# A range test on converted weights: two ScalarE passes with a sum, or one VectorE minimum

## The chip, the cores and the metric

The kernel runs on one core of one Trainium2 chip. Its time is the device time of one execution in microseconds (us). Three runs of the kernel before took 1075.24, 1077.2 and 1079.67 us, median 1077.2. A profile records one execution: the span is the time from its first to its last instruction, and the execution's own time is a little longer.

## The reference

The reference is an attention over hash buckets, followed by a Fourier mixing block with a small network. Reshapes and the bridge between the blocks are left out here.

```python
# q, k, v: (4, 8, 768, 64); proj: (64, 6)
q_bits = (einsum('bhsd,dk->bhsk', q, proj) > 0)          # k_bits likewise
bucket = sum(bits * 2 ** arange(6))
scores = where(q_bucket == k_bucket, q @ k.T / sqrt(64), -1e9)
x = softmax(scores) @ v                                  # to (4, 768, 512)

mixed = real(fft(fft(x, axis=1), axis=2))
u = x + mixed
un = (u - mean(u)) / sqrt(var(u) + 1e-6)
out = u + maximum(un @ w_ch1, 0) @ w_ch2                 # (512, 2048), (2048, 512)
```

The inputs w_ch1 and w_ch2 are float64. The kernel gets them as 64-bit integers and must turn them into float32 itself.

## The kernel before

**Stages.** The four batches are worked through one after another. In each, eight heads are taken as four pairs, and a pair's 768 keys as six chunks of 128. A chunk is scored on TensorE (L909), passed through exp on ScalarE (L922), masked on VectorE by comparing buckets (L936), summed on VectorE (L1043) and multiplied with the values on TensorE (L947). After a pair, the sums go to VectorE for a reciprocal (L979 to L982), are spread by small ScalarE copies (L990), turned back on VectorE (L995) and applied (L999). The mixing block of a batch (`mix`) then folds x on VectorE (L1124 to L1142), does the two Fourier steps on TensorE (L1164, L1193) and runs the network `mlp7`. While one batch is in its mixing block, the attention of the next is interleaved with it.

**The network.** Both matrix products are done with seven block products instead of eight (Strassen and Winograd). `inner` computes the hidden layer: for each of eight rows f it runs the seven products (L1473). ScalarE copies the results out of PSUM (L1513, L1516, L1523, L1528, L1532, L1540), and VectorE adds them up (L1517, L1524, L1529, L1533, L1541). ScalarE's Relus (L1496) are held back and issued right behind later copies. PSUM has two banks for these products, so a late copy stops TensorE. For batch 0 the left operands come from w1 in SBUF, and `quarters` (L1266 to L1269) prepares those of the next row on VectorE. `outer7` does the second product (L1352) with additions on VectorE (L1337, L1338, L1364, L1372, L1380, L1398 to L1404) and copies on ScalarE (L1371, L1382, L1385).

**The weights.** A float64 is two 32-bit words. `narrow` makes float32 out of a slice of 128x512 raw values: VectorE shifts and masks the high words (L639, L643), ScalarE scales the low words (L647), and VectorE adds the two (L649 or L652). The result is only right for numbers within the range of float32, so the kernel tests the range. If the test or another check fails, the whole computation is repeated by a slower general path, `_any_scores`, behind a branch at the end. In the kernel before, the test is two ScalarE instructions (L654 and L655): the absolute value of the high word as a number, and the Relu of a limit minus that value, summed over the slice into one column of the tile `strange`. Any sum above zero means that a word lies below the limit. L654 overwrites the high words in place when there is no other room, as for w2, so it comes behind VectorE's L643, which reads them.

w1 has 16 slices, converted while batch 0's attention runs. w2 has 16 slices as well (`weights2`), two for each step of `inner` of batch 0, and each half of them in one pass through `inner`. Two raw buffers are refilled by POOL's DMA queue (L704) as they come free. After every second slice VectorE forms four more blocks out of the converted ones (L1318 to L1321). Near the end, L1627 takes the maximum over `strange`, and it goes into the flag that decides on the branch.

**Order.** A part of the program up to the end of batch 0's attention is issued in the order in which it is written. Everything later is ordered per engine by a planner, which has costs of its own for the instructions and puts each into a fixed place in its engine's queue. `in_turn` makes an instruction follow the latest ones that `done_by` holds for each engine. Each engine then works through its queue strictly in that order and waits where an operand isn't ready.

Of the kernel before, what the change touches and what calls it, by code (L numbers as in the profile page):

```python
# [11 lines left out]
F32 = mybir.dt.float32  # L12
BF16 = mybir.dt.bfloat16
I32 = mybir.dt.int32
I64 = mybir.dt.int64
U32 = mybir.dt.uint32
AF = mybir.ActivationFunctionType
ALU = mybir.AluOpType
AX = mybir.AxisListType
# [5 lines left out]
DFF = 4 * DM  # L25
# [5 lines left out]
NDC = DM // P  # L31
GTT = 2
GT = GTT * P
WC = 512
# [451 lines left out]
def _main(  # L486
# [13 lines left out]
    nc = tc.nc  # L500
# [13 lines left out]
    def wt(shape, dtype, tag, name, bufs=2):  # L514
        return work.tile(shape, dtype, tag=tag, name=name, bufs=bufs)
# [4 lines left out]
    def pt(shape, name):  # L520

        turn[0] += 1
        if roomy[0] and turn[0] % 2:
            if turn[0] % 4 == 1:
                return ps_o.tile(shape, F32, tag="o", name=name)
            return ps_sc.tile(shape, F32, tag="sc", name=name)
        return ps_1.tile(shape, F32, tag="ps", name=name)
# [92 lines left out]
    w2 = const.tile([P, NFC, DM], F32, tag="w2", name="w2")  # L620


    least = const.tile([P, 1], F32, tag="least", name="least")
    nc.gpsimd.memset(least, float(897 << 20))
    strange = const.tile([P, 2 * NDC * DFF // WC], F32, tag="strange", name="strange")
    nc.gpsimd.memset(strange, 0.0)

    def narrow(dst, raw, col, low=None):


        lo, hi = (raw[..., i] for i in range(2))
        t = lo.bitcast(F32)
        if low is None:

            low, t = lo, hi.bitcast(F32)
        di = dst.bitcast(I32)


        nc.vector.tensor_scalar(  # L639
            di, hi, 3, (1 << 30) - 1,  # L640
            op0=ALU.logical_shift_left, op1=ALU.bitwise_and,
        )
        nc.vector.scalar_tensor_tensor(  # L643
            di, hi, -(1 << 30), di, op0=ALU.bitwise_and, op1=ALU.bitwise_or
        )

        nc.scalar.activation(low, lo.bitcast(U32), AF.Copy, scale=2.0**-29)  # L647
        if len(di.shape) == 2:
            nc.vector.tensor_tensor(di, di, low, op=ALU.add)  # L649
        else:  # L650
            for i in range(di.shape[1]):
                nc.vector.tensor_tensor(di[:, i], di[:, i], low[:, i], op=ALU.add)  # L652

        nc.scalar.activation(t, hi, AF.Abs)  # L654
        nc.scalar.activation(  # L655
            t, t, AF.Relu, bias=least, scale=-1.0, accum_out=strange[:, col : col + 1]
        )
# [17 lines left out]
    def centre(f, avg):  # L675
        for c in range(NDC):
            w = w1[:, c, f : f + WC]
            nc.vector.tensor_tensor(w, w, avg, op=ALU.subtract)
# [12 lines left out]
    class Arrival:  # L691
# [19 lines left out]
        def convert(self, i, low=None):  # L711
            if self.wide:
                dst = self.slices[i][0]
                raw = self.raws[i % self.depth].bitcast(I32)
                if len(dst.shape) == 2:
                    raw = raw.rearrange("p (n w) -> p n w", w=2)
                else:
                    raw = raw.rearrange("p (s n w) -> p s n w", w=2, n=dst.shape[-1])
                narrow(dst, raw, self.col + i, low)
            self.fetch(i + self.depth)  # L720
# [570 lines left out]
    def weights2():  # L1291

        slices = []
        for half in range(2):
            for r in range(HF // 2):
                for hi, first in ((0, B11), (1, B21)):
                    c = half * HF // 2 + r + hi * HF

                    step = 1 if hi else T1 - B11
                    dst = w2f[:, 0 : 7 * QB].rearrange("p (i r n) -> p i r n", i=7, n=HD)  # L1300
                    slices.append(
                        (dst[:, first : first + step + 1 : step, r],
                         moe_w_ch2[c * P : (c + 1) * P, :])
                    )
        arrival = Arrival(slices, [zt2[:, i] for i in range(2)], NDC * DFF // WC, nc.gpsimd)
        for half in range(2):
            if half == 0:
                for i in range(arrival.depth):
                    arrival.fetch(i)
                yield  # L1310
            for i in range(HF):
                with in_turn():
                    arrival.convert(half * HF + i)
                yield
                if i % 2:
                    b11, b21, b22, t4, t1, t2, t3 = (q[:, i // 2] for q in right7)
                    with in_turn():
                        nc.vector.tensor_tensor(t3, b22, t1, op=ALU.subtract)  # L1318
                        nc.vector.tensor_tensor(t1, t1, b11, op=ALU.subtract)
                        nc.vector.tensor_tensor(t2, b22, t1, op=ALU.subtract)  # L1320
                        nc.vector.tensor_tensor(t4, b21, t2, op=ALU.subtract)  # L1321
            for i in range(7):
                nc.sync.dma_start(bd[half, i], right7[i])
            if half == 0:
                yield
# [240 lines left out]
    def after(n, one, two):  # L1566

        for i, _ in enumerate(one):
            if i >= n and (i - n) % 2 == 0:
                next(two, None)  # L1570
            yield
        for _ in two:
            pass
# [28 lines left out]
    for b in range(B):  # L1602
        if b > 0:

            wait = 0
            if b == 1:
                next(other)
                next(other)  # L1610
                wait = 2
            steps, done = NPAIR * NT - wait, 2 if b == 1 else 0
            for i, _ in enumerate(attention(b), 1):
                if b == 1 and i == 2:
                    for f, avg in means:
                        centre(f, avg)
                while done * steps < (MIX - LEFT) * (i - wait):
                    next(other)
                    done += 1
        if b == B - 1:  # L1620
            roomy[0] = True

            ms = const.tile([P, 3], F32, tag="ms", name="ms")
            nc.vector.tensor_reduce(ms[:, 0:2], norms, axis=AX.X, op=ALU.max)
            nc.vector.tensor_reduce(ms[:, 2:3], strange, axis=AX.X, op=ALU.max)  # L1627
            ps = pt([1, 3, P], "norms_t")
            for io in range(3):
                nc.tensor.transpose(ps[:, io, :], ms[:, io : io + 1], ident)  # L1630
            mt = const.tile([1, 5], F32, tag="mt", name="mt")
            nc.vector.tensor_reduce(mt[:, 0:3], ps, axis=AX.X, op=ALU.max)
            nc.vector.tensor_tensor(mt[:, 3:4], mt[:, 0:1], mt[:, 1:2], op=ALU.mult)
            nc.vector.tensor_scalar(
                mt[:, 4:5], mt[:, 3:4], (SAFE / SCALE / 2) ** 2, None, op0=ALU.is_gt
            )
            fl = const.tile([1, 1], I32, tag="fl", name="fl")
            nc.vector.scalar_tensor_tensor(
                fl, mt[:, 2:3], 0.0, mt[:, 4:5], op0=ALU.is_gt, op1=ALU.max
            )  # L1640
            large = nc.values_load(fl[0:1, 0:1], min_val=0, max_val=1)
        for _ in other:
            pass
        other = mix(b)
        if b == 0:
            zt2 = wt([P, 3, 2 * WC], F32, "z", "zraw2", 1)
            arrival2 = weights2()
            other = after(NT, other, islice(arrival2, HF + 2))
# [6 lines left out]
def kernel(tc, *args):  # L1655

    cn = {n: tc.nc.inline_tensor(a, name="k_" + n) for n, a in _consts().items()}
    with ExitStack() as ctx:
        large = _main(ctx, tc, *args, cn)
    with tc.If(large > 0, preferred_fallthrough_block=True):  # L1660
        _any_scores(tc, *args, cn)
# [34 lines left out]
```

## Time and profile before

| what | value |
|---|---|
| median of three runs | 1077.2 us (1075.24 to 1079.67) |
| the profiled execution | 1077.68 us |
| its span | 1075.9 us |
| TensorE busy | 1035.8 us, 96% |
| VectorE busy | 779.1 us, 72% |
| ScalarE busy | 500.7 us, 47% |
| L654, one of w2's | 0.688 us on ScalarE |
| L655, one of w2's, and its accumulator read | 0.777 and 0.190 us on ScalarE |
| first and last L639 of w2's slices | 153.1 and 338.2 us |

In the profile's lines PE is TensorE, PEld its weight loads, DVE VectorE, ACT ScalarE, POOL GpSimd and SP the engine that issues most transfers. L654 is line 654 of the kernel before. A line gives output and inputs by the program's names, the shape, and how often it ran ("x16"). What stands in brackets is idle time in front of an instruction and what ended it. A matmul in fp32 leaves two records, and some are missing.

### The profile page before, as it was taken

The numbers are of one execution on the slowest core, as the hardware profiler recorded it, in microseconds if no ns is written. First come the engines' busy times: TensorE is split into PE (matmuls) and PEld (weight loads), VectorE is DVE, ScalarE is ACT, GpSimd is POOL, SyncE is SP. The second block draws the span as 40 slices with busy tenths as digits, with TensorE's granted clock in tenths as the row PEclk, the third lists the DMA queues.
The fourth block names the chain that finished last, engine by engine and source line by source line (L and its number), as shares of the span: only waits on it lengthen the run. The fifth ranks groups of instructions, "written<-read, shape, count | busy, mean of one in ns | idle before, by whom it ended". The sixth has DMA issues, their size and how long they took to land.

```text
span 1075.9 us, 14182 instructions
## 1 busy us (share of the span) xinstructions
PE 1035.8 (96%) x4965; PEld 633.6 (59%) x4965; DVE 779.1 (72%) x1326; ACT 500.7 (47%) x1057; POOL 59.1 (5%) x132
## 2 busy tenths in 40 slices
PE   7999899999999999999999999999999999999996
PEld 3333364447644585546664575655675579668575
DVE  5788969896799967877758877776856875644353
ACT  7888564762387324455336425354325522440420
POOL 0000000011000020010000020010000012200000
PEclk9999999999999999999999999999999999999999
DMA  8754551380154461224062232322032204222301
GB/s 206 201 140 86 104 141 46 124 238 6 32 142 158 139 195 24 56 62 87 12 198 71 66 116 98 55 64 65 16 119 91 65 25 171 65 74 98 118 20 42
DMA packets 175710, 103.13 MB, mean 96 GB/s; under 512 B 129552, under 2 KB 162960, under 8 KB 175632
## 3 DMA queue, kind: packets, MB, share of 16 engines
q1 hardware_dynamic: 169840, 88.65, 30.4%
q0 software_dynamic: 4224, 13.11, 3.8%
q8 instruction: 41, 0.67, 0.3%
q10 hardware_dynamic: 1568, 0.39, 0.2%
q14 instruction: 37, 0.30, 0.1%
HBM read 81.14 MB, written 20.97 MB: 95 GB/s over the span
## 4 chain that ended last, share of the span: by engine, by line
PE 77%; DVE 12%; ACT 6%; issue 2%; DMA 2%; SPq 2%; DVEq 0%; ACTq 0%
PE o L1352 26%; PE h_p L1473 22%; PE oo L947 10%; PE sc L909 9%; PE cs L1164 3%; DVE pk L936 2%; ACT pk L922 2%; PE A L1193 2%; DVE acc L1043 2%; PE B L1193 1%; DMA kn<-in_k_dram 1%; SPq L576 1%; PE sum L957 1%; DVE x L1207 1%; PE bits L838 1%
## 5 line engine op out<-in xcount | busy, mean ns | idle before, releaser
L1352 PE MATMUL o<-w,h 128*128 128x256 f32 x1152 | 259.4, 382 | 0.8 <-DVE w L1364 0.5
L1352 PEld LDWEIGHTS o<-w,h 128*128 128x128 f32 x1152 | 217.4, 191 | 42.0 <-issue 5.8
L922 ACT ACTIVATE pk<-sc 128x768 f32<-128x768 f32 x192 | 147.0, 808 | 77.1 <-PE oo L947 34.6
L1473 PE MATMUL h_p<-x,w 128*128 128x384 f32 x448 | 164.4, 494 | 3.1 <-ACT w L1540 1.7
L909 PE MATMUL sc<-qt,kt 64*128 64x384 f32 x768 | 154.6, 505 | 3.1 <-ACT pk L922 2.8
L936 DVE SCALAR_TENSOR_TENSOR pk<-qb,kb,pk 128x768 f32<-128x768 bf16 x132 | 128.7, 1011 | 38.2 <-ACT pk L922 38.1
L947 PE MATMUL oo<-pk,vn 128*64 128x385 f32 (+1 forms) x768 | 146.2, 495 | 0.8 <-DVE pk L936 0.6
L1473 PEld LDWEIGHTS h_p<-x,w 128*128 128x128 f32 x448 | 82.1, 190 | 69.0 <-issue 9.3
L1473 PE MATMUL h_p<-w 128*128 128x384 f32 x288 | 106.1, 490 | 0.1
L1043 DVE TENSOR_TENSOR acc<-acc,pk 128x1536 f32<-128x1536 f32 (+1 forms) x64 | 98.5, 1549 | 5.4 <-ACT pk L922 5.2
L947 PEld LDWEIGHTS oo<-pk,vn 128*64 128x64 f32 x768 | 50.5, 136 | 86.3 <-issue 73.1
L909 PEld LDWEIGHTS sc<-qt,kt 64*128 64x128 f32 x768 | 66.5, 187 | 57.2 <-issue 20.2
L1473 PEld LDWEIGHTS h_p<-w 128*128 128x128 f32 x288 | 53.6, 190 | 39.6 <-ACT w L1528 2.4
L1382 ACT COPY tq<-o 128x256 f32<-128x256 f32 x24 | 8.9, 372 | 104.3 <-PE o L1352 104.3
L1364 DVE SCALAR_TENSOR_TENSOR w<-o,rs,w 128x256 f32<-128x256 f32 x56 | 26.6, 479 | 41.2 <-PE o L1352 41.2
L1487 ACT ACTIVATE h<-h 128x384 f32<-128x384 f32 x72 | 37.4, 524 | 24.4 <-DVE h L1529 10.4
L1352 PE MATMUL o<-w 128*128 128x256 f32 x176 | 42.2, 383 | 0.2 <-DVE w L1364 0.2
L1524 DVE TENSOR_TENSOR h<-h 128x384 f32<-128x384 f32 x32 | 17.7, 554 | 29.6 <-ACT h L1523 29.6
L1102 POOL DMA_DIRECT2D out_dram<-w x30 | 16.3, 546 | 407.6 <-issue 314.6
L1352 PEld LDWEIGHTS o<-w 128*128 128x128 f32 x176 | 32.9, 190 | 7.5 <-DVE w L1364 1.2
L1371 ACT COPY tq<-o 128x256 f32<-128x256 f32 x24 | 8.8, 368 | 60.3 <-PE o L1352 60.2
L1398 DVE TENSOR_TENSOR tq<-tq,o 128x256 f32<-128x256 f32 x24 | 10.0, 417 | 36.4 <-PE o L1352 36.4
(171 smaller groups left out, 1316.9 us busy)
## 6 DMA issues: line engine op xcount, KB each, us to landing
w<-ad SPq DMA_DIRECT2D x168, 128.0 KB, 2.0
w<-bd SPq DMA_DIRECT2D x42, 512.0 KB, 4.4
zraw<-in_moe_w_ch_dram POOLq DMA_DIRECT2D x16, 512.0 KB, 3.9
bd<-w SPq DMA_DIRECT2D x14, 512.0 KB, 4.4
vn<-in_v_dram SPq DMA_DIRECT2D x32, 192.0 KB, 3.3
qn<-in_q_dram SPq DMA_DIRECT2D x120, 48.0 KB, 2.4
kn<-in_k_dram SPq DMA_DIRECT2D x60, 96.0 KB, 3.1
zraw<-in_moe_w_ch_dram SPq DMA_DIRECT2D x8, 512.0 KB, 7.1
```

Of the source, the lines that this page charges most:

```text
L909: last[0] = nc.tensor.matmul(ps[:, h, 0:HALF], kt[rows, ks], qt[rows, qs], start=kb is not None or early, stop=not early,)
L922: done_by[ET.Activation] = nc.scalar.activation(pk[:, g, :, 0:HALF], ps[:, :, 0:HALF], AF.Exp, scale=SCALE)
L936: done_by[ET.DVE] = nc.vector.scalar_tensor_tensor(w, qb[:, h].rearrange("p (g s) -> p g s", g=2), kb[:, h, c : c + 1], w, op0=ALU.is_equa ...
L947: oo = nc.tensor.matmul(oos[g][h * D : (h + 1) * D, 0:w], nat["v", n][:, (2 * c + h) * D : (2 * c + h + 1) * D], pk[:, g, h, 0:w], start=( ...
L1043: done_by[ET.DVE] = nc.vector.tensor_tensor(acc[:, g], (first if c == 1 else acc)[:, g], new[:, g], op=ALU.add,)
L1164: nc.tensor.matmul(ps[:, pc + 2 * lo : pc + 2 * hi - 1 : 2], z[:, cp, pc, par, t * P : (t + 1) * P], ch[:, cp, pc, lo:hi], start=(cp == 0) ...
L1193: nc.tensor.matmul(ps[:, cols], F[:, par, k, t, j * P : (j + 1) * P], sq[:, t, k, cols], start=(t == 0), stop=(t == 1),)
L1352: nc.tensor.matmul(ps, a[:, r], right7[i][:, r], start=start and r == 0, stop=r == HF // 2 - 1, skip_group_check=not start,)
L1364: nc.vector.scalar_tensor_tensor(t[:, cols], src, r, t[:, cols], op0=ALU.mult, op1=ALU.add)
L1473: nc.tensor.matmul(ps, left[:, k], right[i][:, k], start=start and k == 0, stop=k == 1, skip_group_check=not start,)
L1487: done_by[ET.Activation] = nc.scalar.activation(h, h, AF.Relu)
L1524: done_by[ET.DVE] = nc.vector.tensor_tensor(c22, c21, c22, op=ALU.add)
```

## The change

For w2's slices the two ScalarE instructions go. In their place VectorE takes one reduction over the high words of the slice, read as float32: the minimum of the absolute values, written into the slice's column of `strange`. It writes nothing over the raw words. The limit is now the same bit pattern read as float32. For w1's slices the two ScalarE instructions stay, but read the high words as float32 too. At the end, w2's 16 columns hold minima and no sums, so one comparison turns each into 1 (below the limit) or 0 before the maximum is taken.

```diff
+    LEAST = float(np.int32(897 << 20).view(np.float32))
     least = const.tile([P, 1], F32, tag="least", name="least")
-    nc.gpsimd.memset(least, float(897 << 20))
+    nc.gpsimd.memset(least, LEAST)
...
-        nc.scalar.activation(t, hi, AF.Abs)
+        if col >= NDC * DFF // WC:
+            nc.vector.tensor_reduce(
+                strange[:, col : col + 1], hi.bitcast(F32), axis=AX.XY,
+                op=ALU.min, apply_absolute_value=True,
+            )
+            return
+        nc.scalar.activation(t, hi.bitcast(F32), AF.Abs)
         nc.scalar.activation(
             t, t, AF.Relu, bias=least, scale=-1.0, accum_out=strange[:, col : col + 1]
         )
...
             nc.vector.tensor_reduce(ms[:, 0:2], norms, axis=AX.X, op=ALU.max)
+            if moe_w_ch2.dtype == I64:
+                low = strange[:, NDC * DFF // WC :]
+                nc.vector.tensor_scalar(low, low, LEAST, None, op0=ALU.is_lt)
             nc.vector.tensor_reduce(ms[:, 2:3], strange, axis=AX.X, op=ALU.max)
```

## The prediction

> **What bounds the kernel now.** I read the page first: which engine is nearest to full.
>
> ```profile
> span 1075.9 us, 14182 instructions
> PE 1035.8 (96%) x4965; PEld 633.6 (59%) x4965; DVE 779.1 (72%) x1326; ACT 500.7 (47%) x1057; POOL 59.1 (5%) x132
> ```
>
> TensorE is the bound over the whole span, so only what lengthens or shortens TensorE's gaps counts. The 16 slices of w2 are converted between 150 and 343 us, so I next asked for busy time by stretches around them (columns: stretch, its length, busy us and instructions of PE, PEld, DVE, ACT, POOL, then granted clock, DMA share, GB/s).
>
> ```profile
> 192.00:204.00 12.00, 10.69 (x38) 5.24 (x36) 11.86 (x25) 8.50 (x20) 0.92 (x2) 1.00 0.45 143
> 307.00:336.00 29.00, 25.30 (x89) 12.44 (x88) 28.64 (x59) 23.91 (x53) 2.11 (x4) 1.00 0.47 140
> 342.00:361.00 19.00, 18.50 (x85) 11.93 (x84) 18.71 (x36) 7.31 (x15) 0.55 (x1) 1.00 0.44 173
> 361.00:400.00 39.00, 37.14 (x175) 28.75 (x174) 31.21 (x63) 10.96 (x28) 6.98 (x14) 0.96 0.54 147
> ```
>
> The averages mislead here. In the first three stretches VectorE is full (11.86 of 12, 28.64 of 29, 18.71 of 19) and TensorE is not. The last stretch has a granted clock of 0.96: 39 x 0.04 = 1.6 us lost. Third, the chain that ended last, to see what the ScalarE test has to do with it (start, length, what):
>
> ```profile
> 322.12 0.61 DVE w L643
> 322.75 0.71 ACT zraw L654
> 323.48 0.85 ACT zraw L655 x2
> 324.33 0.37 ACT h L1516
> 324.73 0.56 DVE h L1517
> ```
>
> The old test (L654, L655) stands on the chain in front of a copy that empties a PSUM bank. Such pieces start at 194.22, 224.93, 322.75 and 340.96 us; their L654 and L655 parts are 0.58+0.74, 0.63+0.86, 0.71+0.85 and 0.61, together 5.0 us. Fourth, TensorE's timeline, for what released it:
>
> ```profile
> 204.49 1.56 PE L1473 MATMUL h_p<-x,w 128*128 128x384 f32 x4 [1.71 <-ACT w L1540]
> 324.75 1.56 PE L1473 MATMUL h_p<-bt,tq 128*128 128x384 f32 x4 [1.33 <-ACT h L1516]
> 335.46 1.53 PE L1473 MATMUL h_p<-bt,tq 128*128 128x384 f32 x4 [0.49 <-DVE tq L1267]
> 372.95 1.64 PE L909 MATMUL sc<-qt,kt 64*128 64x384 f32 x4 [1.59 <-ACT pk L922]
> ```
>
> 324.75 is pure ScalarE delay. At 204.49 ScalarE is only the messenger: its copy L1540 stands behind the Relu L1496, which waited for VectorE's L1529. At 335.46 VectorE releases TensorE itself.
>
> [...] L639 takes 0.41 us for 512 elements, the two-input L643 0.68. Its only reductions are tiny: 0.18 us for 32 elements (L1627), 0.50 for 3x128 from PSUM (L1632). [...] the trace's 128x512 adds take 0.68. [...] Here the 0.96 stretch begins with the 1.59 us wait at 372.95, so a broken supply costs about that much again; but the 1.71 us wait at 204.49 cost no clock.
>
> **The change part by part.** Removed: 16 times L654 (0.688), L655 (0.777) and its accumulator read (0.190), 1.655 us each, 26.5 us of ScalarE. Also removed are the waits of L654 for L643 (9.0 us, 6 times), with which everything behind it on ScalarE waited. Their worth on the chain is the 5.0 us above, if nothing else holds the same place.
>
> Added: 16 reductions of 128x512 fp32 words at stride two on VectorE. Price: the 128x512 statistics L1225 take 0.68 us and follow each other at 0.60 (242.46 after 241.86); so do L643 and the adds. Lower end 0.34, the spacing of L639[...]. I take 0.60, so 9.6 us in all. The comparison on 128x16 and the changed constant cost about 0.1 us in a place with no one waiting. For w1 the two ScalarE instructions stay, reading the same words under another type: nothing.
>
> Moved: refills of the raw buffers (16 on POOL's queue) no longer wait for L655 but for conversion and reduction. They stay hidden: a refill lands after 3.9 us, and ScalarE's L647 waited for data only twice (3.1 us in all, the first two slices). If that cover went, each late slice would cost up to 3.9 us. No DMA is added; on SP a few loads and buffer reads change places. The program's order of instructions is identical up to 150 us and again from about 430; between, VectorE, ScalarE and TensorE are reordered.
>
> Now by stretch, with slices counted from 0.
>
> 150 to 180: slices 0 and 1. VectorE idles 0.56 us before L936 and 0.59 before L979 right behind them, and 0.60 falls into each. Zero.
>
> 186 to 250: slices 2 to 7. Idle of 0.64 (slice 2), 1.27 (5), 0.64 and 0.37 (6), 0.40 (7) takes theirs, with 0.2 left over. Slices 3 and 4 find none: VectorE runs without a hole from 191.67 to the L1529 that frees L1496, L1540 and TensorE at 204.49. That is 2 x 0.60; the new order also puts L1529 (0.47) and L1266 (0.34) of the preceding step behind the hole at 191, less about 0.3 of small gaps. 1.2 + 0.8 - 0.3 = 1.7. With the 0.2: +1.9. Removing L654 and L655 gains nothing at 194: L1517 would start after L936 anyway, 0.07 us earlier.
>
> 250 to 290: TensorE full, VectorE 45 to 80%. Zero.
>
> 290 to 361: slices 8 to 15. Slices 8 and 9 add 1.2 before the reciprocal L982, on which the next exponentials depend, while L1267 and L1269 (0.72) move behind it: +0.4 with rounding. Slices 10 to 14 are 5 x 0.60 = 3.0 in the full stretch up to L1267 at 335. Slice 15 adds 0.6. In return two L1129 and one L1337 (0.47+0.47+0.60 = 1.5) move behind the L1364 that releases TensorE at 359.08. 0.4+3.0+0.6-1.5 = +2.5. The ScalarE waits of this stretch (1.33 at 324.75, 0.88, 0.30) vanish, but TensorE then reaches VectorE's L1267 earlier and waits there longer.
>
> 361 to 430: at 370 eight small copies (L990, 1.67 us) stand between two exponentials and cause the 1.59 wait and the clock drop. In the new order four exponentials go ahead of them: up to 1.6 + 1.6 = 3.2 us back. Against it, four chunks of attention move from 401-421 into 372-397: eight L936, two sums and two transposes, about 12 us of VectorE beside 12 us of TensorE work, in a stretch where VectorE had 7.8 us idle and now brings a backlog. I keep 1.0 of the 3.2.
>
> Sum: 1.9 + 2.5 - 1.0 = +3.4 us. The profiled execution took 1077.7 us (span 1075.9, 1.8 around it), so 1081.1; it stood 0.5 above the median of the three runs, 1077.2, so against that median 1080.6 us. No difference that this kernel's measurement can tell from none is 0.5%, 5.4 us here: 1071.8 to 1082.6.
>
> **The rivals.** A: ScalarE's relief decides, and it ends faster. The place is the copies L1513, L1516 and L1528, which empty PSUM behind the test; the price is the 5.0 us on the chain, and with the 3.2 at 370 it gives 1069.0. For it: ScalarE was 24 of 29 us busy at 307 to 336, and TensorE's largest wait there was behind L655. Against it: VectorE had under 0.4 us idle there. It decides if fewer than 8 of the 16 reductions lengthen VectorE's path (8 x 0.60 = 4.8); I count ten.
>
> B: the delay feeds on itself. The waits near 204 and 337 grow to 3 us and more, each brings a half-clock window (1.6 each), and the crowded 372 to 397 gives nothing back but loses 2: 1.9+2.5+3.2+2.0 = 9.6, 1086.8 us. For it: the drop at 373 after 1.59 us. Against it: none after 1.71 us at 203, and the new order puts scores and values (2.9 us) ahead of the wait at 335.
>
> C: the reduction is cheap (0.34). Then slices 3 and 4 cost 1.2, the 290 to 361 stretch about 0.5 (2.0 less the 1.5 moved away), 370 gives back 1.0: +0.7, 1077.9 us. [...]
>
> That the change doesn't do what it says: the built program has 16 reductions and no L654, L655 for w2, so no.
>
> **How the numbers follow.** Forecast 0.42 (own range 1078 to 1084), A 0.20, B 0.27, C 0.11. Faster than 1071.8: most of A, 0.17. Slower than 1082.6: B and the upper tenth of the whole from the forecast, 0.37. The rest 0.46. For 8 in 10 I leave out 0.1 below (half of A) and 0.1 above (the far part of B): 1070.5 to 1088.
>
> **What would show it.** Right: reductions near 0.68 us each, 11 us busy for 16; ScalarE busy about 26 us less; VectorE full from 307 to about 340; TensorE's wait before L1473 near 205 grown to 3 us and still behind L1540; no 0.88 to 1.33 waits behind L1516 and L1528; clock 1.00 at 370 to 380. Wrong: VectorE with holes in 307 to 340 (then A), reductions of 0.4 (C), new slices of lower clock (B), or a refill for which L647 waits.

## The result

| | us |
|---|---|
| before, median of six runs beside the changed kernel | 1077.12 (1075.24 to 1079.67) |
| after, median of six runs | 1084.16 (1082.66 to 1086.34) |
| ratio | 1.0074, interval 1.0062 to 1.0086 |
| predicted | 1080.6 (1070.5 to 1088.0) |

The change makes the kernel 7.0 us slower. That is inside the range, which is 17.5 us wide, and on the side of the sum, which gave +3.4; half of the loss is missing from it. The profiled execution after took 1084.77 us; its span is 7.1 us longer than before.

The page of the kernel after begins so (span, then busy time, share and instructions of each engine):

```profile
span 1083.0 us, 14167 instructions
PE 1038.2 (96%) x4965; PEld 633.6 (59%) x4965; DVE 787.9 (73%) x1343; ACT 479.1 (44%) x1009; POOL 59.1 (5%) x132
```

ScalarE lost 21.6 us, VectorE gained 8.8. The minimum itself, in the list of the costliest groups of VectorE (count, busy us, mean ns of one):

```profile
L656 DVE TENSOR_REDUCE strange<-zraw 128x1 f32<-128x512 f32 x16 | 10.9, 681 | 0.0
```

Busy time by stretches, kernel after, with the columns of the view shown before (of the pairs, the third is VectorE and the fourth ScalarE; behind POOL's pair stands the granted clock):

```profile
192.00:204.00 12.00, 10.83 (x38) 5.11 (x36) 12.00 (x25) 5.38 (x12) 0.53 (x1) 1.00 0.37 124
307.00:336.00 29.00, 25.91 (x84) 13.69 (x83) 27.73 (x56) 16.69 (x38) 2.11 (x4) 0.94 0.47 144
336.00:361.00 25.00, 23.66 (x106) 11.90 (x104) 23.78 (x48) 10.80 (x21) 0.00 (x0) 1.00 0.49 184
361.00:400.00 39.00, 35.74 (x176) 24.01 (x173) 39.00 (x71) 13.81 (x31) 4.29 (x8) 1.00 0.28 60
```

ScalarE now has slack everywhere. VectorE is full in the first row and nearly so in the next two (27.73 of 29 and 23.78 of 25 us). The news is the last row: VectorE, 31.21 of 39 us before, has no hole left, and TensorE fell from 37.14 to 35.74. (TensorE is 2.5 to 5.5 us late in the last three rows, so they don't hold quite the same work as before.) The clock is 1.00 there now; the lowered clock stands in the second row, 29 x 0.06 = 1.7 us. TensorE's timeline of the kernel after (start, us, what, in brackets the wait and what ended it):

```profile
206.17 1.56 PE L1480 MATMUL h_p<-x,w 128*128 128x384 f32 x4 [2.09 <-ACT w L1547]
...
324.56 2.90 PE L1480 MATMUL h_p<-bt,tq 128*128 128x384 f32 x4 [2.28 <-DVE tq L1274]
...
341.90 2.77 PE L954 MATMUL oo<-pk,vn 128*64 128x385 f32 x8 [0.58 <-DVE pk L943]
...
396.93 3.29 PE L1359 MATMUL o<-w,h 128*128 128x256 f32 x14 [2.43 <-DVE w L1371]
```

(Lines above 661 have moved by 7: L1480 was L1473, L1547 L1540, L1274 L1267, L954 L947, L1359 L1352, L1371 L1364.) The first wait grew from 1.71 us. The 1.33 behind ScalarE's L1516 is gone: the group that waited there, at 324.75, now starts at 328.80 without a wait. Two groups ahead of it, at 324.56, TensorE waits 2.28 behind VectorE, where it had no wait before. The row at 341.90 is a chunk of attention that ran behind the products before; its eight matmuls take 2.7 us where such a row takes 1.5, because the second four wait for the second mask of L943, which ends at 343.1. The fourth wait is new. What VectorE did before it, from the chain that ended last (start, length, what):

```profile
387.22 0.93 DVE pk L943
388.14 0.94 DVE ef L1136 x2
389.08 0.93 DVE pk L943
390.01 1.07 DVE z L1145 x4
391.08 0.08 DVE z L1149
391.16 0.92 DVE pk L943
392.08 0.87 DVE ef L1131
392.95 0.93 DVE pk L943
393.88 0.94 DVE ef L1136 x2
394.81 1.67 DVE acc L1050
396.48 0.41 DVE w L1371
```

L1371, which the network's second product waits for, comes last, behind four masks (L943) and a sum (L1050) of the next batch's attention and the folding of x (L1131, L1136, L1145).

**Where the 7 us arise.** I take the start of each group of TensorE's matmuls and subtract that of the same group in the profile before; the offset at 120 us is taken off. These delays are the measure in all that follows; they are read at places that have the same work of TensorE ahead of them in both kernels:

| kernel | to 290 us | 290 to 362 | 362 to 430 | 430 to 1060 | sum |
|---|---|---|---|---|---|
| after | +2.5 | +2.9 | +0.6 | +0.6 | +6.7 |

The rest of the 7.1 lies in the last stores.

### The profile page after: what moved, and what is told of

Read it like the earlier page. It is cut to its first block, busy times and chain, and to the rows that moved or that the text cites. A ratio compares the mean times of both kernels' runs of the same rounds, so it can differ in the third digit from the quotient of the medians.

```text
span 1083.0 us, 14167 instructions
## 1 busy us (share of the span) xinstructions
PE 1038.2 (96%) x4965; PEld 633.6 (59%) x4965; DVE 787.9 (73%) x1343; ACT 479.1 (44%) x1009; POOL 59.1 (5%) x132
## 4 chain that ended last, share of the span: by engine, by line
PE 72%; DVE 17%; ACT 6%; issue 2%; DMA 2%; SPq 0%; DVEq 0%; ACTq 0%
PE o L1359 25%; PE h_p L1480 20%; PE oo L954 9%; PE sc L916 8%; DVE pk L943 3%; PE cs L1171 3%; ACT pk L929 2%; DVE acc L1050 2%; PE A L1200 2%; PE B L1200 2%; PE sum L964 1%; DVE x L1214 1%; DVE w L653 1%; DMA kn<-in_k_dram 1%; DVE w L644 1%
## 5 line engine op out<-in xcount | busy, mean ns | idle before, releaser
L1359 PE MATMUL o<-w,h 128*128 128x256 f32 x1152 | 258.7, 381 | 3.3 <-DVE w L1371 2.4
L1359 PEld LDWEIGHTS o<-w,h 128*128 128x128 f32 x1152 | 216.6, 190 | 43.9 <-issue 5.8
L1480 PE MATMUL h_p<-x,w 128*128 128x384 f32 x448 | 164.8, 495 | 4.7 <-ACT w L1547 2.1
L943 DVE SCALAR_TENSOR_TENSOR pk<-qb,kb,pk 128x768 f32<-128x768 bf16 x132 | 129.2, 1012 | 33.5 <-ACT pk L929 33.4
L954 PE MATMUL oo<-pk,vn 128*64 128x385 f32 (+1 forms) x768 | 148.0, 495 | 1.8 <-DVE pk L943 1.6
L1480 PEld LDWEIGHTS h_p<-x,w 128*128 128x128 f32 x448 | 82.2, 190 | 71.7 <-issue 9.5
L1480 PE MATMUL h_p<-w 128*128 128x384 f32 x288 | 106.1, 490 | 0.1
L954 PEld LDWEIGHTS oo<-pk,vn 128*64 128x64 f32 x768 | 51.0, 136 | 88.8 <-issue 72.1
L1050 DVE TENSOR_TENSOR acc<-acc,pk 128x1536 f32<-128x1536 f32 (+1 forms) x64 | 98.6, 1550 | 5.4 <-ACT pk L929 5.2
L1480 PEld LDWEIGHTS h_p<-w 128*128 128x128 f32 x288 | 53.6, 190 | 39.6 <-ACT w L1535 2.4
L1371 DVE SCALAR_TENSOR_TENSOR w<-o,rs,w 128x256 f32<-128x256 f32 x56 | 26.6, 480 | 38.5 <-PE o L1359 38.5
L1359 PE MATMUL o<-w 128*128 128x256 f32 x176 | 42.3, 383 | 0.2 <-DVE w L1371 0.2
L1359 PEld LDWEIGHTS o<-w 128*128 128x128 f32 x176 | 32.9, 190 | 8.0 <-issue 1.6
```

Of the source, the lines that this page charges most:

```text
L943: done_by[ET.DVE] = nc.vector.scalar_tensor_tensor(w, qb[:, h].rearrange("p (g s) -> p g s", g=2), kb[:, h, c : c + 1], w, op0=ALU.is_equa ...
L954: oo = nc.tensor.matmul(oos[g][h * D : (h + 1) * D, 0:w], nat["v", n][:, (2 * c + h) * D : (2 * c + h + 1) * D], pk[:, g, h, 0:w], start=( ...
L1050: done_by[ET.DVE] = nc.vector.tensor_tensor(acc[:, g], (first if c == 1 else acc)[:, g], new[:, g], op=ALU.add,)
L1359: nc.tensor.matmul(ps, a[:, r], right7[i][:, r], start=start and r == 0, stop=r == HF // 2 - 1, skip_group_check=not start,)
L1371: nc.vector.scalar_tensor_tensor(t[:, cols], src, r, t[:, cols], op0=ALU.mult, op1=ALU.add)
L1480: nc.tensor.matmul(ps, left[:, k], right[i][:, k], start=start and k == 0, stop=k == 1, skip_group_check=not start,)
```

## The experiments

Times are medians beside runs of the kernel before on the same chip. Delays are of one profiled execution each. TensorE's granted clock differs between executions (0.994 to 0.999 in the six of the changed kernel), so its median is given, and the median of time x clock, which takes the lost cycles out (before: 0.998 and 1074.0); it takes out too much where a drop falls into a time in which TensorE would have waited anyway. The column "pulled" says whether the planner ran the chunks of attention early, at 339 and at 372 to 397 us, as it does in the changed kernel.

| kernel | minima | pulled | us | ratio to before | clock | us x clock | to 290 | 290 to 362 | 362 to 430 |
|---|---|---|---|---|---|---|---|---|---|
| after | 16 | both | 1084.2 | 1.0074 | 0.997 | 1080.2 | +2.5 | +2.9* | +0.6 |
| none | 0 | no | 1075.5 | 0.9999 | 0.997 | 1072.9 | +1.2* | -0.6 | -1.6 |
| half | 16 of half size | no | 1075.8 | 0.9991 | 0.998 | 1074.0 | +1.5 | +0.1 | -3.1 |
| split | 16 of half size | no | 1076.4 | 1.0005 | 0.998 | 1074.5 | +1.6 | +0.3 | -3.1 |
| not34 | 14 | both | 1083.0 | 1.0057 | 0.996 | 1078.7 | +1.3 | +2.9 | +0.6 |
| two | 32 | both | 1088.8 | 1.0108 | 0.995 | 1083.5 | +4.2* | +6.7* | +1.0 |
| first11 | 11 | no | 1081.6 | 1.0048 | 0.996 | 1076.9 | +2.5 | +0.3 | -1.6 |
| last6 | 6 | both | 1083.3 | 1.0056 | 0.995 | 1077.4 | +1.3* | +2.5 | +2.3* |
| late | 16 | no | 1083.1 | 1.0061 | 0.995 | 1077.7 | +2.2 | +5.7* | -3.1 |
| free | 16 | no | 1079.3 | 1.0023 | 0.996 | 1074.9 | +4.4* | +2.5* | -3.1 |
| held339 | 16 | no | 1080.4 | 1.0045 | 0.997 | 1077.2 | +2.5 | +2.1* | -2.9 |
| held372 | 16 | at 339 | 1084.3 | 1.0081 | 0.995 | 1078.4 | +4.1* | +2.9* | +1.6* |
| held380 | 16 | in part | 1083.1 | 1.0063 | 0.995 | 1077.7 | +4.1* | +2.9* | -1.1 |

(* A drop of the clock fell into this stretch in the profiled execution. In the profile before it lasts 3.41 us, from 373.0 to 376.4, at a granted clock of 0.50, and in that after as long, from 324.3 on, at 0.50 too: at most 1.7 us of TensorE's work. The other profiles fit: 44 x 0.04 = 1.8 us in `none` from 206 to 250. The drop of the kernel before cost 1.6 us between 362 and 430, so -1.6 there means only that it didn't come.)

Where no chunk is pulled at 372 to 397 there are still two orders. `before`, `none` and `first11` score two chunks of the next batch at 368 to 376 us and wait there for 1.59 to 1.68 us (L909 before). In `half`, `split`, `late`, `free`, `held339` and `held372` these 16 matmuls stand behind the second product, from 393 us on, and that wait is gone. `held380` leaves them in place, with a wait of 0.27.

### What is ScalarE's relief worth: no test at all

```diff
         if col >= NDC * DFF // WC:
-            nc.vector.tensor_reduce(
-                strange[:, col : col + 1], hi.bitcast(F32), axis=AX.XY,
-                op=ALU.min, apply_absolute_value=True,
-            )
             return
```

> No range test for w2 at all: neither the two ScalarE instructions nor the VectorE minimum, nor the comparison at the end. The planner gives TensorE the order of the kernel before but for three rows. This isolates what taking the test off ScalarE is worth. My theory (VectorE binds where the weights are converted): little, 1074.5 to 1077.5 us, because VectorE's queue holds the same places; of the ScalarE waits of 1.33, 0.88 and 0.30 us before the first product's matmuls up to about 1.5 us come back, and the 1.59 us wait at 373 stays. Rival (ScalarE's relief is real and the minima eat it and 7 us more): 1069 to 1072 us, so that the minima cost 12 to 15 us in all.

Measured: 1075.53 us, ratio 0.9999 (0.9988 to 1.0009). The relief is worth nothing that these runs can tell, some 1.3 us at most; rival A falls. In this order of TensorE, then, no form of the test should be much faster than the old one. For other orders this run sets no bound: the next two kernels get back 1.5 us more than this one from 362 on. TensorE's timeline of this kernel shows why the relief is worth so little. The waits of 0.88, 1.33 and 0.30 behind ScalarE's L1528 and L1516 are gone, and this stands in their place:

```profile
204.80 1.57 PE L1476 MATMUL h_p<-x,w 128*128 128x384 f32 x4 [2.19 <-ACT w L1543]
...
336.61 1.53 PE L1476 MATMUL h_p<-bt,tq 128*128 128x384 f32 x4 [2.51 <-DVE tq L1270]
...
373.89 0.92 PE L912 MATMUL sc<-qt,kt 64*128 64x384 f32 x4 [1.68 <-ACT pk L925]
```

The wait for VectorE's quarters (L1270 here) is 2.51 us in place of 0.49: what ScalarE gave, VectorE's queue kept. At 204 ScalarE is still only the messenger: the Relu ahead of L1543 had waited 3.00 us for VectorE. The wait at 373 stayed, as expected.

### Half the work: half and split

`half` takes the minimum over 256 of a slice's 512 words. `split` does the same, and ScalarE tests the other half, so that the test is whole (its sums go into a tile of their own, `rest`, which joins the maximum at the end; not shown):

```diff
+            n = hi.shape[-1] // 2
             nc.vector.tensor_reduce(
-                strange[:, col : col + 1], hi.bitcast(F32), axis=AX.XY,
+                strange[:, col : col + 1], hi[..., 0:n].bitcast(F32), axis=AX.XY,
                 op=ALU.min, apply_absolute_value=True,
             )
+            t, hi = t[..., n:], hi[..., n:]            # from here on split only
+            nc.scalar.activation(t, hi.bitcast(F32), AF.Abs)
+            nc.scalar.activation(
+                t, t, AF.Relu, bias=least, scale=-1.0, accum_out=rest[...],
+            )
             return
```

> The minimum is taken over half of each slice's words only (256 of 512 elements, the rest is not tested): the same 16 instructions at about 0.33 us each in place of 0.60. The planner's order for TensorE is then nearly that of the kernel before (16 rows differ, against 58 between before and after). Theory 'amount' (what counts is VectorE time in its full stretches): about half of the loss, 1079.5 to 1081.5 us, with the delay near 204 us at +1.0 in place of +1.7. Rival 'order' (what costs is the order the planner chose after 290 us): 1077 to 1078.5 us, the loss being only what arises before 290.

> The whole test, nothing left out, in two parts: the minimum on VectorE over one half of each slice (0.33 us), the two ScalarE instructions with the sum on the other half (256 words, about 0.48 and 0.57 us and the accumulator read of 0.19), into a column of its own. TensorE's order is the one of the kernel with half-size minima, row for row. Theory: ScalarE's relief is worth nothing and half a minimum fits, so this is as the half test: 1075 to 1077 us, no difference from before. Rival (ScalarE's part on the path costs again): 1078 to 1080 us.

Measured: 1075.84 us (0.9991, 0.9983 to 1.0000) and 1076.41 us (1.0005, 0.9996 to 1.0013). Half the reduction is not half the loss: it costs nothing. Both theories expected more: "amount" by 4 us, "order" by 1. The delays say how: +1.5 before 290, as both allowed, but then -3.1 from 362 to 430, where the changed kernel loses 0.6. That is the 3.2 that the prediction had seen at 370 and mostly written off, whole: the wait of 1.59 and the drop of the clock are both gone (`half`: 1.00 from 361 to 400 us). ScalarE's half costs nothing that shows (the ratios of the two kernels overlap).

### The step at 204: not34

```diff
-        if col >= NDC * DFF // WC:
+            if col - NDC * DFF // WC not in (3, 4):
                 nc.vector.tensor_reduce(...)
```

> The changed kernel without the minimum on slices 3 and 4 (these two are not tested). TensorE's and ScalarE's orders stay those of the changed kernel. My prediction charged 1.7 us to this place: 1.2 for the two minima and 0.5 for two additions that changed places. Theory: TensorE's delay at 204 to 206 us is +0.3 to +0.6 in place of +1.7, and the time 1082.5 to 1083.2 us, since nothing between 206 and 290 gets it back. Rival (slack later absorbs it): delay gone at 206, but the time again 1084 us. Rival (the changed places of the additions are the cause): delay stays at +1.2 or more.

Measured: delay at 206 us +0.5 after the offset; TensorE's timeline:

```profile
205.29 1.56 PE L1482 MATMUL h_p<-x,w 128*128 128x384 f32 x4 [1.52 <-ACT w L1549]
```

Up to 290 us the two minima are worth 2.5 - 1.3 = 1.2 us, 2 x 0.60 to the digit. The time fell to 1083.04 us, 1.1 less, as expected, though the intervals of the two ratios overlap. By the delays nothing later gets it back.

### Twice the work: two

```diff
             nc.vector.tensor_reduce(strange[:, col : col + 1], ...)
+            nc.vector.tensor_reduce(strange[:, col : col + 1], ...)
```

> Every minimum is taken twice: 32 in place of 16. The planner's order for TensorE stays that of the changed kernel in most rows (33 differ). Theory 'amount': 16 more minima at 0.60 us, of which those of slices 3, 4 and 8 to 15 and some of the others lengthen the path: +6 to +9.6 us, 1090 to 1094 us; TensorE's delay at 206 us becomes +3 to +3.5. Rival 'order' (the loss came with the new order, and VectorE has room elsewhere): 1084 to 1087 us.

Measured: 1088.77 us, 4.6 above the changed kernel, between the two theories. From 290 to 362, where VectorE is nearly full in the changed kernel already (27.73 of 29 us from 307 to 336), it behaves as "amount" says: 3.8 more than the changed kernel. The 1.7 more before 290 can't be read so, since a drop of the clock at 172 us had put it 1.6 behind already; the delay of 3.5 at 206, within the expectation, holds that drop too. From 362 on, where the order decides, it is much the changed kernel's loss again, +1.0.

### Amount or order: first11 and last6

The minimum for slices 0 to 10 only, or for slices 10 to 15 only (the condition on `col` as above; the rest isn't tested). The first keeps the old order of TensorE, the second has the new one.

> The minimum is taken for slices 0 to 10 only (11 of 16; 11 to 15 are not tested). The planner then keeps TensorE's order of the kernel before but for 8 rows, also after 290 us. Theory 'order' (the loss after 290 us comes with the order that the planner chooses once it sees too much VectorE work there): the delay before 290 us is +2.5 as in the changed kernel, 290 to 360 adds 1 to 2, the stretch from 360 to 430 gives back about 3 as it did without a test; 1076 to 1078.5 us. Rival 'amount': 11 of 16 minima, 11/16 of the 8.3 us that lie between half and whole size and no order, so 1081 to 1083 us.

> The minimum is taken for slices 10 to 15 only (6 of 16; 0 to 9 are not tested). The planner then gives TensorE the order of the changed kernel but for 3 rows. Theory 'order': the delay before 290 us is that of the kernel without a test, +1.2 to +1.4; 290 to 360 us adds about 3 and 360 to 430 gives nothing back; 1080.5 to 1082.5 us, more than with eleven minima in the old order. Rival 'amount': 6 of 16 minima, 1077 to 1078.5 us, less than with eleven.

Measured: 1081.58 and 1083.29 us. By their medians six minima cost more than eleven, which "amount" cannot give, but the intervals of the ratios overlap. `first11` lies in the range of its rival, 3 us above what "order" expected; `last6` is 0.8 above its own and far from the rival's. The profiled execution of `first11`, 1079.05 us at a clock of 0.998, is the fastest of five; the others stood at 0.994 to 0.997. So the median is partly lost clock and doesn't settle it; the delays do. From 290 to 430 us `first11` is at -1.3 and `last6` at +4.8. Of the 6.1 between them a drop of the clock is at most 1.7: `last6` has one there (0.96 from 361 to 400 us), as the kernel before has (0.96), and `first11` none (1.00). The timeline of `last6` has the two waits of the changed kernel although it has none of the first ten minima:

```profile
340.18 2.77 PE L956 MATMUL oo<-pk,vn 128*64 128x385 f32 x8 [2.15 <-DVE pk L945]
...
395.22 4.97 PE L1361 MATMUL o<-w,h 128*128 128x256 f32 x14 [2.44 <-DVE w L1373]
```

### The whole test in other orders: late and free

Each minimum is issued one step of the network later, behind it the refill of the raw buffer (`late`), or in the same step but not tied to follow the network's latest instructions (`free`).

```diff
                 with in_turn():
                     arrival.convert(half * HF + i)     # without minimum and refill
+                arrival.least(half * HF + i)           # free: here, not in turn
                 yield
+                with in_turn():
+                    arrival.least(half * HF + i)       # late: here
```

> All 16 minima at full size, nothing left out, but each is issued one step of the network later than its conversion, and the refill of the raw buffer behind it. TensorE's order then differs from that of the kernel before in 30 rows and is not that of the changed kernel (52 rows). Theory 'order': 1076 to 1079.5 us, with the 1.6 to 3 us at 360 to 430 given back. Rival 'amount': as the changed kernel, 1083 to 1085 us. If the later refill matters, the scaling of the low words waits for data and the time is above 1085 us.

> All 16 minima at full size, nothing left out; each is no longer tied to follow the latest instructions of the network, so that the planner may place it by its data alone. Differs from TensorE's order before in 84 rows, some of them already ahead of 200 us. Theory 'order': the time goes with what the planner does at 360 to 430 us: 1076 to 1081 us. Rival 'amount': 1083 to 1085 us.

Measured: 1083.12 and 1079.26 us. Both give back 3.1 us from 362 to 430, as "order" has it, with all 16 minima at full size. `free` has 4.9 us less than the changed kernel. `late` missed its range all the same, and its time lies in the rival's: it pays 5.7 from 290 to 362, more than any other kernel with 16 minima. Why its place is worse there stays open.

### Holding the pulled chunks: held339, held372, held380

One more rule on the changed kernel's order: TensorE's attention instructions of some steps may not overtake the network's products written before them (steps 23 and 24 of batch 1, 1 and 2 of batch 2, or 3 and 4 of batch 2).

```diff
+    def held_back(steps):
+        for i in range(1, 1000):
+            with (
+                tc.issue_after(newest[0].ins)          # the latest product
+                if newest[0] is not None and 23 <= i <= 99 else nullcontext()
+            ):
+                if next(steps, steps) is steps:
+                    return
+            yield
...
-            for i, _ in enumerate(attention(b), 1):
+            for i, _ in enumerate(held_back(attention(b)) if b == 1 else attention(b), 1):
```

> All 16 minima at full size, nothing left out. The last two attention steps of batch 1 (of 24) may no longer overtake, on TensorE, the products of the network written before them. TensorE's order is then that of the changed kernel up to 339 us; the chunk of attention that the planner had pulled to 339 to 344 goes back behind the products, and what follows up to 430 us is, without anything else being asked, the order that the kernel with half-size minima had. Theory 'order': delay before 290 us +2.5 as in the changed kernel, 6 to 8 at 337, and 3 to 6 given back from 345 to 400; 1077 to 1080.5 us. Rival 'amount' (16 minima in full stretches cost what they cost): 1083 to 1085 us.

Measured: 1080.42 us (1.0045, 1.0033 to 1.0058), within the expectation and 3.7 below the changed kernel; by the ratios to the kernel before it is 0.29%, 3.1 us. Two steps of attention in another place, and two fifths to a half of the loss is gone. Busy time of this kernel by stretches:

```profile
290.00:345.00 55.00, 50.79 (x193) 24.85 (x192) 53.57 (x105) 31.54 (x66) 3.26 (x6) 0.97 0.50 140
361.00:400.00 39.00, 38.45 (x186) 29.67 (x182) 33.31 (x73) 9.19 (x25) 8.12 (x16) 1.00 0.54 153
```

In 361 to 400 VectorE has 5.7 us idle, where the changed kernel has none, and TensorE does 38.45 us of work in place of 35.74. Holding the chunk at 339 itself gains 0.8 (2.1 against 2.9); most, 3.5 us, comes from 362 to 430, where the planner's order changed with it. That order is the one of `half`, with nothing else asked, so this run shows that the order costs this much with all 16 minima in place, but not which of the moves does.

> All 16 minima at full size, nothing left out. Only the first two attention steps of batch 2 are held back behind the products written before them. TensorE's order is then that of the changed kernel up to 365 us, the pulled chunk at 339 included; the four chunks that it had pulled from 401 to 421 to 372 to 397 go back to where they were before. This parts the two places. Theory (the crowd at 372 to 397 took the 3.2 us that 370 could give back): delay at 362 us +5.4 as in the changed kernel, +2.3 to +4 from 430 on, 1080 to 1081.5 us. Rival (those chunks only change places and the loss was made by 345 us): again +5.5 to +6 at 430 us, 1083 to 1084.5 us.

Measured: 1084.27 us; by its time the rival is right. By its trace, not so plainly. The delay was 7.0 us at 362 and 0.0 at 395. Some 3.1 of that is no gain, since the 16 scoring matmuls now come behind 395; when they are done, at 400 us, the delay is 3.6. So 3.4 had been given back, as the theory had it, and then a new wait came. ScalarE's timeline, and behind it TensorE's:

```profile
404.51 0.84 ACT L779 ACTIVATE sq<-qn 128x768 bf16<-128x768 f32 x1 [3.62 <-DMA kn<-in_k_dram]
```

```profile
406.74 1.32 PE L1182 MATMUL cs<-ch,z 128*128 128x127 f32 x8 [3.18 <-ACT F L1195]
```

A square over freshly loaded rows, which heads ScalarE's queue, waited for its load; the copy L1195 that TensorE needs stood behind it. The held steps had dragged their loads past the reloads of w2 on SP's queue: the loads of k were issued from 398.3 us on, behind seven reloads, and from 385.4 in the changed kernel. A drop of the clock followed that wait (0.96 from 400 to 440 us). So the total of this run parts nothing; its first 40 us in this stretch speak for the theory.

> All 16 minima at full size, nothing left out. As the run with two steps of batch 2 held back, but steps 3 and 4 are held in place of 1 and 2: the first two chunks' scores stay where the changed kernel has them, the chunks behind them go back from 377 to 397 to after the second product. In the run before, the held steps had taken seven reloads of w2 past the next loads of q and k on SP's queue; here the loads stay ahead of the reloads but for one of k. That run had given back everything by 395 us and then lost 3.18 us and a half-clock window to a late load. Theory (the crowd at 372 to 397 costs about 3 us): no ScalarE wait for a load over 1 us, TensorE's delay +2.3 to +4 us from 430 us on, 1080 to 1082 us. Rival (the chunks only change places, the loss was made by 345 us): +5 to +6 us, 1083 to 1084.5 us.

Measured: 1083.12 us, delay +6.3 with a clock drop before 250 us (0.96 from 206 on) that the profile of the changed kernel hasn't; from 362 to 430 us -1.1 in place of +0.6. Not pulling the four chunks is worth 1.7 of the 3.5, about half of what the theory said. ScalarE's wait for a load was 2.2 us, where I had expected less than 1. By time and total it is the rival's; by the stretch, where the drop doesn't count, the theory is right for half of its amount.

## Why the prediction was right, and where it wasn't

**The price, 0.60 in a row and 0.68 alone: right.** 681 ns is the mean; in the chain the minima take 0.59 to 0.60. None came near the 0.34 after which the next instruction follows an L639: rival C was no case.

**ScalarE's relief hidden behind VectorE: right, and shown** by the kernel without a test. The removal was put at 26.5 us of ScalarE's time, a sum of durations, and 21.6 was measured (20.5 without a test): as a sum it overstated what the engine gave up. That costs nothing here, since ScalarE wasn't the bound.

**To 290 us: +1.9 forecast, +2.5 measured.** The 1.7 at 204 came as worked out (+1.7 at 206, the wait 2.09 and not 3), and its 2 x 0.60 is shown by `not34`. The 0.2 for slices 6 and 7 was mis-sized: +0.8 between 230 and 237, at the same place in `not34` and `first11`, and not in `last6`, which leaves these minima out. There, at 234.80, TensorE waits 0.39 us for the masks (L943), and its row of products with the values takes 2.23 us in place of 1.90. The masks are 2.5 us later than before. The minimum of slice 6, at 216.48, stands right ahead of the addition L1529 (L1536 in the changed kernel), for which ScalarE's Relu at 217.66 waits 1.98 us; the exponentials behind it and their masks are then 2.2 late. The holes of 0.64 and 0.37 that I had set against slice 6 lie behind that addition. Slice 7 adds the 0.2 that was forecast.

**290 to 361: +2.5 forecast, +2.9 measured.** `last6` has +2.5 with the last six minima alone, `first11` +0.3 with slices 8 to 10 (in another order of TensorE): nearly all of it belongs to the last six, much as the sum had it (0.4 for slices 8 and 9, 3.0 + 0.6 - 1.5 for the rest). The drop of the clock at 324 (1.7 us) cost nothing on top: `not34` has +2.9 too, in an execution without a drop (0.999 over the span). So VectorE set the pace there.

**361 to 430: -1.0 forecast, +0.6 measured. This step failed**: "I keep 1.0 of the 3.2". The 3.2 was the right size, and it did come back: in the changed kernel the wait of 1.59 at 373 and the drop of the clock behind it are gone. But new waits of 0.50, 2.43, 0.33 and 0.44 us, the largest the one behind VectorE at 396.93, took 3.7. The prediction allowed the crowded stretch 2.2. Its own working could have said more: 12 us of VectorE were to move into a stretch with 7.8 us idle, which is 4.2 too much, without the backlog, and 4.2 - 3.2 is +1.0, not -1.0. That sum is made afterwards and takes VectorE's overflow as TensorE's loss; it fits, but no run tests it.

**After 430: nothing forecast, +0.6 and the tail 0.5 measured.** At 564 us TensorE waits 0.34 us for ScalarE's L1530, in an order identical to before; `not34` and `last6`, with the same order there, have 0.0. So it seems to belong to that execution. No errors cancelled: all five parts came out higher than forecast, by 3.7 us together, and the number was right because the range was wide enough.

**Rival B** had the mechanism half. The wait at 324 did grow to 2.28 us and a drop of the clock came with it (from 324.3 us), but it cost nothing; of the crowded 372 to 397 it was true that nothing is left of what came back, and its further 2 us lost were 0.6. Lower clocks than in the profile (0.996) came in part of the runs: two of the six executions of the changed kernel, at a clock of 0.994, took 1086.2 and 1086.3 us, the four others at most 1084.8.

What stays open: why the planner turns from one order to another with the minima, and how the 3.5 us parts between the chunks pulled to 372 to 397 (1.7 by `held380`) and the two chunks' scores that go behind the second product.

## What to carry to other kernels

Where a planner decides the order, an instruction added to a full engine has two prices: its length on the path, and what the planner then moves. For each piece that it moves, add the piece's demand on every engine to the stretch it moves into, and let the sum run over. Before making an operation cheaper, leave it out: here that would have shown first that hardly anything was to be won by it in the order that the kernel had.

## What I had not expected of the hardware

The drop of TensorE's clock doesn't follow from the length of the wait alone. 1.59 us at 373 (before) and 2.19 at 204 (none) were followed by one, 1.68 at 373 (none) and 2.09 at 206 (after) were not: the granted clock was 0.83 from 370 to 380 us before and 1.00 without a test, and 1.00 from 204 to 212 after. Busy time of the kernel without a test, around both places:

```profile
206.00:250.00 44.00, 43.24 (x182) 22.96 (x181) 39.12 (x73) 23.50 (x50) 6.41 (x11) 0.96 0.60 182
...
361.00:400.00 39.00, 37.05 (x182) 29.27 (x181) 32.64 (x66) 11.05 (x28) 7.18 (x15) 1.00 0.54 149
```

These runs don't show what else decides it.

Executions of one kernel differ in their clock too: beside the kernel without a test, the kernel before ran 14 times at a clock of 0.998 or more, median 1075.3 us, and 14 times below, median 1077.2, about one drop apart. So of two kernels 2 us apart, compare the clocks first.
